# Second expert layer by row halves at full width, 12 tokens in a row per partition, and a renumbered planner table

## The chip, the cores and the metric

The kernel runs on one core of a Trainium2 chip, in one launch. The metric is device time in microseconds of that launch. Engines are named as the profile names them: PE multiplies matrices (PEld is its loading of the stationary operand), DVE and ACT are the vector and the scalar engine, POOL is the general one, and SP issues every transfer between HBM and the on-chip memory, on one queue.

## The reference

Sliding-window attention with four sink positions feeds a soft mixture of experts. There are 4 batches of 8 heads, 768 positions and 64 channels, so x has 3072 tokens of 512 channels; there are 8 experts with 4 slots each and 1024 hidden channels.

```python
scores = scale * np.matmul(q, k.transpose(0, 1, 3, 2))
keep = is_sink | in_window                     # first 4 positions, or the last 128
a = softmax(np.where(keep, scores, -1e9))      # over keys
x = (a @ v), laid out as (B * S, H * D)        # 3072 x 512
logits = x @ phi                               # 3072 x 32 slots
d = softmax(logits, over tokens)
slot_input = (d.T @ x).reshape(E, 4, D)
for e in range(E):
    slot_out[e] = np.maximum(slot_input[e] @ w1[e], 0.0) @ w2[e]
c = softmax(logits, over slots)
out = c @ slot_out                             # 3072 x 512
```

Everything is float32. The weights w1 and w2 are 16.8 MB each, and the output is 6.3 MB.

## The kernel before

**Two stages.** The attention stage walks over 12 jobs: batch b and a block j of 256 positions, three blocks to a batch. For a job it loads 256 positions of k, q and v (each in two transfers of 256 KB, called halves here), transposes k and q on PE, multiplies scores for four tiles, takes maxima on DVE and exponentials on ACT, normalises on POOL, transposes the result, masks it on POOL, multiplies it with v and with the sink values, and adds the block to the running sums of the slot inputs. The tail then multiplies the 32 slot inputs with w1, applies the rectifier, transposes, multiplies with w2 and combines for all tokens.

**Order.** The attention stage is written as a list of steps, each with a key, an engine, an estimated time, what it reads and what it writes. `Plan.order` (lines 165 to 246) replays the list on a model of five engines: of the steps of an engine that could start now it takes the one with the smallest key. The keys come from the table CFG (lines 671 to 690), most of them as 4n plus an entry for job n. The order found this way is the program order of each engine. For the queue "D", that is SP, the steps are the loads of k, q, v, the gate phi, the sink values v4, and 17 weight tiles. Weight step i has the key `O["w"][0] + O["w"][1] * i` (line 994) and depends on nothing; the loads of job n have keys `4.0 * n + O["load"][kind]` and `4.0 * n + O["v"][i]`. The k and q of job 0 are issued at line 1165, ahead of all this. The first products on PE are warm-up on the identity.

**Weights.** `Weights.load` issues one transfer of 1 MB (1,048,576 bytes) into a slot of 128 partitions x 2048 floats, in a fixed order of 32 tiles: 16 tiles of w1, then 16 of w2. A w1 tile has runs of 4 KB in HBM. A w2 tile is one expert with 256 of the 512 columns, so its runs are 1 KB; first the left halves of all eight experts, then the right ones. Tiles 1 to 17 go out in the attention stage (NSLOT is 24), one into the buffer first[0] when the last q and k have been used, four into slots as the attention stage frees them, one into first[1], and nine more from within the tail (`more`), as the w1 tiles are used up.

**Second layer and output.** The four experts of a row half r sit side by side in PE's four column groups of 32 (j), so four matmuls run at once; k counts the eight parts of the hidden channels. Before, the 512 output columns are done as three strips s0 (256 columns), s1 and s2 (128 each): for each strip 16 steps over r and k (`second`), a split of the result into a high part and a remainder (`split`), and the combination with the slot weights ct for 24 groups of 128 tokens (`combine`), four groups to a store. Group i holds tokens 128 i + p on partition p, so a store has runs of 1 KB (s0) or 512 B (s1, s2). `turned` transposes the last six units of ct between steps. Tiles of a strip's combination and steps of the next strip are interleaved by hand. An instruction that is issued through the ordering helper is recorded at line 127.

Of the kernel before, what the change touches and what calls it, by code (L numbers as in the profile page):

```python
# [8 lines left out]
F32 = mybir.dt.float32  # L9
# [5 lines left out]
ALU = mybir.AluOpType  # L15
# [4 lines left out]
P = 128  # L20
# [251 lines left out]
class Moe:  # L272
# [246 lines left out]
    def tail(self, slot, wts, more, out):  # L519
        nc, c, B, si, pool = self.nc, self.c, self.B, self.si, InOrder(self.pools)  # L520
# [40 lines left out]
        ops = [pool.tile("s") for _ in range(2)]  # L561
        tw = slot().bitcast(F32R)[:, 0:1024].rearrange("p (x m) -> p x m", x=2)
        obs = [slot() for _ in range(3)]
        ov = out.rearrange("(i p) m -> p i m", p=P)

        def op(s):
            return ops[s[0] == 256][:, s[0] > 256, 0:s[1]]

        def second(s, r, k0=0, k1=8):
            c0, m = s  # L570
            h, o = divmod(c0, 256)
            for k in range(k0, k1):
                for j in range(4):
                    nc.tensor.matmul(op(s)[32 * j:32 * j + 32],
                                     lhsT=ht[:, k, r, j].rearrange("p q i -> p (q i)"),
                                     rhs=wts[16 + 8 * h + 4 * r + j][:, 256 * k + o:256 * k + o + m],
                                     start=(r == 0 and k == 0), stop=(r == 1 and k == 7), skip_group_check=True)

        def split(s):
            c0, m = s  # L580
            hi, x = tw[:, 0, c0:c0 + m], op(s)
            nc.scalar.copy(hi, x)
            nc.vector.scalar_tensor_tensor(tw[:, 1, c0:c0 + m], hi.bitcast(F32), c.lo_rows, x,  # L583
                                           op0=ALU.mult, op1=ALU.add)

        def combine(s, n):
            c0, m = s
            per = 512 // m

            x = n + (6 if c0 == 384 else 0) if m == 128 else 2 * n  # L590
            x, y = divmod(512 * x, 2048)
            ob = obs[x][:, y:y + 4 * m].rearrange("p (i m) -> p i m", i=4)
            for x in range(4 // per):
                yp = pool.tile()
                for y in range(per):
                    i = 4 * n + per * x + y
                    nc.tensor.matmul(yp[:, m * y:m * y + m], lhsT=self.ct[i // 12][:, i // 6 % 2, i % 6, :],
                                     rhs=tw[:, 1, c0:c0 + m], start=(y == 0), stop=(y == per - 1),
                                     skip_group_check=True)
                (nc.scalar.copy if (n * (4 // per) + x) % 2 == 0 else nc.vector.tensor_copy)(  # L600
                    ob[:, per * x:per * x + per, :], yp.rearrange("p (i m) -> p i m", i=per))
            nc.sync.dma_start(ov[:, 4 * n:4 * n + 4, c0:c0 + m], ob)

        s0, s1, s2 = (0, 256), (256, 128), (384, 128)
# [5 lines left out]
        steps = {s: iter([(s, r, k, k + 1) for r in range(2) for k in range(8)]) for s in (s0, s1, s2)}  # L610

        def some(s, n):
            for _ in range(n):
                second(*next(steps[s]))

        def combined(s, *n):
            for x in n:
                combine(s, x)

        for n in range(3):  # L620
            some(s0, 4)
            turned(n)
        some(s0, 4)
        split(s0)
        some(s1, 4)
        combined(s0, 0, 1)
        some(s1, 3)
        turned(3)
        combined(s0, 2, 3)
        some(s1, 3)  # L630
        turned(4)
        combined(s0, 4)
        some(s1, 3)
        turned(5)
        some(s1, 3)
        split(s1)
        combined(s0, 5)
        some(s2, 4)
        combined(s1, 0, 1)
        some(s2, 4)  # L640
        combined(s1, 2, 3)
        some(s2, 4)
        combined(s1, 4)
        some(s2, 4)
        split(s2)
        combined(s1, 5)
        combined(s2, *range(6))


class Weights:  # L650


    def __init__(self, nc, w1, w2):
        self.nc, self.w1, self.tiles = nc, w1, []
        self.order = [(w1, 4 * r + 2 * j, k) for r in range(2) for k in range(4) for j in range(2)]
        self.order += [(w2, e, h) for h in range(2) for e in range(8)]

    def load(self, t):
        w, e, h = self.order[len(self.tiles)]
        first = w is self.w1  # L660
        self.nc.sync.dma_start(
            t.rearrange("p (k m) -> p k m", k=2 if first else 8),
            w[e:e + 2].rearrange("e (k p) m -> p e k m", p=P)[:, :, h, :] if first else
            w[e].rearrange("(p k) m -> p k m", p=P)[:, :, 256 * h:256 * h + 256])
        self.tiles.append(t)


NSLOT = 24
WARM = 8, 10
PT = 3  # L670
CFG = {'prep': [-1.63, -1.96],
       'load': [-6.04, -6.69],
       'v': [-6.3, 0.97],
       'S': -4.67,
       'M': 2.42,
       'E': -3.34,
       'N': 0.29,
       'K0': 1.89,
       'T': [2.6, 6.04, 3.99, 4.25],
       'K': 6.01,  # L680
# [543 lines left out]
```

## Time and profile before

| | us |
|---|---|
| median of 3 runs | 268.26 |
| lowest, highest run | 266.33, 268.53 |
| profiled execution | 266.88 |
| its span | 265.2 |
| attention stage, to the slot inputs (copy of si on DVE) | 0 to 205.1 |
| first layer of the experts on PE | 205.2 to 221.4 |
| last weight tile used from | 240.4 |
| last copy of an output tile ends | 257.2 |

The page gives an execution's busy times, a chain of work that ended last, and groups of instructions. Rows of busy time by stage give the start and end of a stretch, its length, the busy time of PE, PEld, DVE, ACT and POOL in it with the number of instructions, the granted clock of PE (1.00 is full), the mean busy share of the DMA engines and GB/s. Rows of the timeline give start, length, engine, line, operation, what is written and read, and, in brackets, how long the engine stood before and what released it. Rows of waits give the total, the number and the longest. Rows of transfers end with KB and the microseconds from issue to landing. A float32 matmul is recorded twice, once for each of its two passes.

| GB/s by the page's 40 slices | |
|---|---|
| slices 24 to 29 (152 to 192 us) | 42, 119, 77, 124, 2, 42 |
| slices 33 to 37 (212 to 245 us) | 348 to 354, then 318 |
| slices 38 to 40 (245 to 265 us) | 233, 248, 138 |

### The profile page before, as it was taken

The page shows a single profiled execution, that of the slowest core. Times are in us where ns is not written, and L with a number is a line of the kernel's source. Part 1 is how long each engine was busy: PE and PEld are TensorE (multiplying, and loading weights), DVE is VectorE, ACT ScalarE, POOL GpSimd, SP SyncE. Part 2 cuts the span into 40 slices and gives each one's busy share as a digit, 9 for nine tenths or more (in the row PEclk, how much of TensorE's full clock was granted, in tenths as well). Part 3 has the DMA queues.
Part 4 walks back from the last instruction along what each step waited for, and adds up shares of the span by engine and source line. Part 5 has one row for each costly group of instructions (what it writes and reads, how often), then busy time and mean ns, then how long its engine had stood idle before and what let it go on. Part 6 is the DMA issues. An engine that isn't in the chain of part 4 may idle for free.

```text
span 265.2 us, 7578 instructions
## 1 busy us (share of the span) xinstructions
PE 235.4 (89%) x2802; PEld 163.4 (62%) x2802; DVE 173.0 (65%) x449; ACT 147.7 (56%) x578; POOL 141.3 (53%) x280
## 2 busy tenths in 40 slices
PE   7777999979999997999999799998896999977960
PEld 7655686746767684676678566766574225555850
DVE  2287989698889869888986989898415213041340
ACT  2366877577686857678685767767633003142330
POOL 1145989684775958477695847669942040310000
PEclk9979999999999999999999999999998699997995
DMA  7998797988889898589889816340199799999784
GB/s 139 191 197 162 203 269 248 275 172 267 232 259 327 277 235 256 171 167 353 247 271 224 215 42 119 77 124 2 42 288 346 217 351 348 350 354 318 233 248 138
DMA packets 106111, 59.38 MB, mean 224 GB/s; under 512 B 76372, under 2 KB 101972, under 8 KB 106068
## 3 DMA queue, kind: packets, MB, share of 16 engines
q1 hardware_dynamic: 106068, 58.83, 79.5%
q8 instruction: 24, 0.39, 0.6%
q14 instruction: 19, 0.16, 0.2%
HBM read 52.53 MB, written 6.29 MB: 222 GB/s over the span
## 4 chain that ended last, share of the span: by engine, by line
PE 61%; DVE 19%; DMA 5%; ACT 5%; POOL 3%; issue 3%; ACTq 0%; POOLq 0%; DVEq 0%
PE w L127 47%; PE s L127 13%; DVE wt L127 7%; DVE s L127 6%; DMA wt<-in_moe_w_dram 5%; POOL wt L127 3%; ACT wt L127 2%; DVE sums L127 2%; PE w L1176 1%; ACT lt L127 1%; ACT qt L127 1%; DVE call L127 1%; DVE rs L127 1%; DVE acc L127 1%; DVE pst L127 1%
## 5 line engine op out<-in xcount | busy, mean ns | idle before, releaser
L127 POOL TENSOR_TENSOR wt<-wt 128x528 f32<-128x528 f32 (+1 forms) x96 | 64.5, 673 | 27.8 <-DVE wt L127 23.9
L127 ACT ACTIVATE wt<-s,wt 128x132 f32<-128x132 f32 x192 | 68.5, 378 | 11.5 <-DVE wt L127 10.4
L127 POOL TENSOR_SCALAR_AFFINE_SELECT wt<-wt 128x512 f32<-128x512 f32 x88 | 53.8, 635 | 24.5 <-DVE wt L127 15.3
L127 PE MATMUL w<-wt 128*64 128x128 f32 (+4 forms) x586 | 55.0, 315 | 0.3 <-DVE wt L583 0.2
L127 PEld LDWEIGHTS w<-wt 128*64 128x64 f32 (+2 forms) x586 | 40.3, 144 | 12.2 <-issue 1.1
L127 PE MATMUL s<-wt,qt 64*64 64x196 f32 (+2 forms) x768 | 43.7, 331 | 3.5 <-ACT wt L127 2.9
L127 PE MATMUL w<-ident,first 128*128 128x128 f32 x288 | 42.8, 281 | 3.7 <-DVE pst L127 2.8
L127 PE MATMUL w<-ident,wt 128*128 128x128 f32 x256 | 38.5, 280 | 2.9 <-POOL wt L127 2.3
L127 ACT ACTIVATION_READ_ACCUMULATOR wt<-s,wt 128x1 f32 x192 | 40.9, 213 | 0.0
L127 PEld LDWEIGHTS w<-ident,first 128*128 128x128 f32 x288 | 31.9, 142 | 12.2 <-issue 4.8
L127 PEld LDWEIGHTS s<-wt,qt 64*64 64x64 f32 x768 | 27.6, 135 | 15.7 <-ACT wt L127 8.4
L127 ACT COPY first<-w 128x512 f32<-128x512 f32 x36 | 21.2, 589 | 28.1 <-PE w L127 28.0
L127 PEld LDWEIGHTS w<-ident,wt 128*128 128x128 f32 x256 | 28.7, 145 | 10.8 <-POOL wt L127 4.7
L127 DVE TENSOR_REDUCE wt<-s 128x4 f32<-128x528 f32 x48 | 34.0, 707 | 1.6
L127 DVE COPY wt<-w 128x512 f32<-128x512 f32 x46 | 30.3, 682 | 1.9 <-PE w L127 1.7
L127 DVE COPY_PREDICATED s<-later,s 128x256 f32<-128x256 uint8 x48 | 20.3, 422 | 6.4 <-PE s L127 5.8
L127 PE MATMUL s<-wt 128*32 128x128 f32 (+1 forms) x352 | 18.1, 316 | 3.1 <-DMA wt<-in_moe_w_dram 3.1
L127 ACT COPY wt<-w 128x512 f32<-128x512 f32 x26 | 14.9, 593 | 6.2 <-PE w L127 6.0
L127 PE MATMUL w<-wt,si 128*32 128x512 f32 x128 | 16.2, 670 | 0.4 <-DVE si L127 0.4
L127 PEld LDWEIGHTS s<-wt 128*32 128x32 f32 x352 | 11.1, 114 | 7.6 <-DMA wt<-in_moe_w_dram 3.7
L600 DVE COPY wt<-w 128x512 f32<-128x512 f32 x12 | 8.1, 690 | 11.2 <-PE w L127 11.2
L127 DVE MEMSET s<- 64x512 f32 (+1 forms) x16 | 6.2, 385 | 14.0 <-PE s L127 13.3
(109 smaller groups left out, 243.2 us busy)
## 6 DMA issues: line engine op xcount, KB each, us to landing
wt<-in_moe_w_dram SPq DMA_DIRECT2D x30, 1024.0 KB, 7.9
first<-in_k_dram SPq DMA_DIRECT2D x24, 256.0 KB, 4.2
first<-in_q_dram SPq DMA_DIRECT2D x24, 256.0 KB, 4.3
wt<-in_v_dram SPq DMA_DIRECT2D x24, 256.0 KB, 4.2
out_dram<-wt SPq DMA_DIRECT2D x6, 512.0 KB, 5.1
out_dram<-wt SPq DMA_DIRECT2D x12, 256.0 KB, 4.4
first<-in_moe_w_dram SPq DMA_DIRECT2D x2, 1024.0 KB, 6.8
acc<-in_moe_phi_dram SPq DMA_DIRECT2D x1, 64.0 KB, 5.1
```

The costliest lines, as they stand in the source:

```text
L127: return self.tc.keep_in_program_order(f(*args, **kw))
L600: (nc.scalar.copy if (n * (4 // per) + x) % 2 == 0 else nc.vector.tensor_copy)(ob[:, per * x:per * x + per, :], yp.rearrange("p (i m) -> p ...
L1176: nc.tensor.matmul(t[:, 0:P], lhsT=c.ident, rhs=c.ident, start=True, stop=True)
```

## The change

**Second layer.** One accumulation of 128 partitions x 512 columns takes the place of the three strips: 16 steps of four matmuls with 512 columns (64 instructions in place of 192), the six turns of ct after every second step. The result is split in two halves of 256 columns once all steps are done, and the combination starts after that.

**Weight tiles.** The w2 tiles are now row halves: for r = 0 four experts with 8 KB runs (four of the eight parts k, all 512 columns), twice; for r = 1 the first four parts the same way, and the last four parts in four tiles that hold two experts and two parts each, in 4 KB runs. The number of tiles and their size are the same.

**Output.** The tokens of a group are now every twelfth one: partition p of a group i holds token 12 p + i of a half of 1536 tokens, so the stationary operand is `ct[:, i:1536:12]`, and a store of two or four groups has runs of 4 or 8 KB. There are seven stores in place of 18. Each group is two matmuls of 256 columns into one PSUM tile and one copy of 512 columns, on ACT and DVE in turn.

**The planner's table.** All entries of CFG but a few are renumbered. The weight steps' key goes from 9.75 + 16.41 i to 6.04 - 3.67 i; the other entries move the order of PE, DVE, ACT and POOL in the first four of the twelve jobs, and of a few steps later, most of them on POOL.

SP's queue after the branch, before (in_moe_w is w1 or w2, first holds q and k, wt is a slot, acc the gate's phi; "32x1x64" are the sink values):

```order
L127 DMA wt<-in_v_dram 128x8x64
L127 DMA first_76<-in_q_dram 128x8x64 x2
L127 DMA wt<-in_v_dram 128x8x64
L127 DMA first_76<-in_k_dram 128x8x64 x2
L127 DMA acc<-in_moe_phi_dram 128x4x32
L127 DMA wt<-in_v_dram 128x8x64
L127 DMA first_76<-in_q_dram 128x8x64 x2
L127 DMA wt<-in_v_dram 32x1x64 x4
L127 DMA first_76<-in_k_dram 128x8x64 x2
L127 DMA wt<-in_v_dram 128x8x64
L127 DMA first_76<-in_q_dram 128x8x64 x2
L127 DMA wt<-in_moe_w_dram 128x2x1024
```

The same queue from the same place, after:

```order
L127 DMA wt<-in_moe_w_dram 128x2x1024 x13
L127 DMA wt<-in_v_dram 128x8x64
L127 DMA wt<-in_moe_w_dram 128x2x1024
L127 DMA first_76<-in_q_dram 128x8x64 x2
L127 DMA wt<-in_v_dram 128x8x64
L127 DMA first_76<-in_k_dram 128x8x64 x2
L127 DMA wt<-in_moe_w_dram 128x2x1024
L127 DMA acc<-in_moe_phi_dram 128x4x32
L127 DMA first_76<-in_q_dram 128x8x64 x2
L127 DMA wt<-in_v_dram 128x8x64
L127 DMA wt<-in_v_dram 32x1x64 x4
L127 DMA first_76<-in_k_dram 128x8x64 x2
```

The first weight tile moved from the twelfth place to the first, and thirteen of them now stand ahead of job 0's v and job 1's q and k. The keys below those of job 0's loads are those with i from 4 to 16. All other loads keep their order except the sinks, which stand behind one more weight tile.

PE from the first value product of job 0 on, before (w<-wt 128x256 is the product that spreads the sink values, pst,vsink and wt 64x256 the value product; w<-ident,first are transposes of k or q, w<-ident,wt of exponentials, s<-wt,qt scores):

```order
L127 MATMUL w<-ident,first_76 128x128 x8
L127 MATMUL s<-wt,qt 64x196 x8
L127 MATMUL w<-wt 128x256
L127 MATMUL s<-wt,qt 64x196 x8
L127 MATMUL w<-ident,wt 128x128 x6
L127 MATMUL s<-wt,qt 64x196 x8
L127 MATMUL w<-pst,vsink 128x256 x2
L127 MATMUL w<-wt 64x256 x2
```

After:

```order
L127 MATMUL w<-ident,first_76 128x128 x4
L127 MATMUL s<-wt,qt 64x196 x8
L127 MATMUL w<-ident,wt 128x128 x10
L127 MATMUL w<-wt 128x256
L127 MATMUL w<-ident,first_76 128x128 x8
L127 MATMUL w<-pst,vsink 128x256 x2
L127 MATMUL w<-wt 64x256 x2
```

The four score tiles of job 1 and ten transposes now all stand ahead of the sink product, and between it and the value product stand the eight transposes of job 2's k.

SP's end of the queue, before:

```order
L127 DMA first_76<-in_moe_w_dram 128x8x256
L127 DMA wt<-in_v_dram 128x8x64 x2
L127 DMA wt<-in_moe_w_dram 128x8x256 x4
L127 DMA first_77<-in_moe_w_dram 128x8x256
L127 DMA wt<-in_moe_w_dram 128x8x256 x9
L602 DMA out_dram<-wt 128x4x256 x6
L602 DMA out_dram<-wt 128x4x128 x12
```

After:

```order
L127 DMA first_76<-in_moe_w_dram 128x2048
L127 DMA wt<-in_v_dram 128x8x64 x2
L127 DMA wt<-in_moe_w_dram 128x2048 x4
L127 DMA first_77<-in_moe_w_dram 128x2048
L127 DMA wt<-in_moe_w_dram 128x2048 x5
L127 DMA wt<-in_moe_w_dram 128x2x1024 x4
L606 DMA out_dram<-wt 128x1024 x2
L606 DMA out_dram<-wt 128x2048 x5
```

The weight tiles keep their places and change their shape; the stores are fewer and larger.

The diff, cut:

```diff
-        ops = [pool.tile("s") for _ in range(2)]
+        op = pool.tile("s")[:, 0, :]
...
-        def second(s, r, k0=0, k1=8):
-            c0, m = s
-            h, o = divmod(c0, 256)
-            for k in range(k0, k1):
-                for j in range(4):
-                    nc.tensor.matmul(op(s)[32 * j:32 * j + 32],
-                                     lhsT=ht[:, k, r, j].rearrange("p q i -> p (q i)"),
-                                     rhs=wts[16 + 8 * h + 4 * r + j][:, 256 * k + o:256 * k + o + m],
...
+        def second(r, k):
+            t = 16 + 8 * r + 4 * (k // 4)
+            for j in range(4):
+                if t < 28:
+                    w = wts[t + j][:, 512 * (k % 4):512 * (k % 4) + 512]
+                else:
+                    o = 1024 * (j % 2) + 512 * (k % 2)
+                    w = wts[28 + 2 * (k % 4 // 2) + j // 2][:, o:o + 512]
+                nc.tensor.matmul(op[32 * j:32 * j + 32], lhsT=ht[:, k, r, j].rearrange("p q i -> p (q i)"), rhs=w,
+                                 start=(r == 0 and k == 0), stop=(r == 1 and k == 7), skip_group_check=True)
...
+        for r in range(2):
+            for k in range(8):
+                second(r, k)
+                if k % 4 in (1, 3) and 4 * r + k // 2 < 6:
+                    turned(4 * r + k // 2)
+        for h in range(2):
+            o = slice(256 * h, 256 * h + 256)
+            hi, x = tw[:, 0, o], op[:, o]
+            nc.scalar.copy(hi, x)
+            nc.vector.scalar_tensor_tensor(tw[:, 1, o], hi.bitcast(F32), c.lo_rows, x, op0=ALU.mult, op1=ALU.add)
+        n = 0
+        for x in range(2):
+            ct = self.ct[x].rearrange("p b i y -> p (b i y)")
+            ov = out[1536 * x:1536 * x + 1536].rearrange("(p i) m -> p i m", i=12)
+            for i0, i1 in ((0, 2), (2, 4), (4, 8), (8, 12)) if x == 0 else ((0, 4), (4, 8), (8, 12)):
+                ob = slot()[:, 0:512 * (i1 - i0)].rearrange("p (i m) -> p i m", i=i1 - i0)
+                for i in range(i0, i1):
+                    yp = pool.tile()
+                    for h in range(2):
+                        o = slice(256 * h, 256 * h + 256)
+                        nc.tensor.matmul(yp[:, o], lhsT=ct[:, i:1536:12], rhs=tw[:, 1, o],
+                                         start=(h == 0), stop=(h == 1), skip_group_check=True)
+                    (nc.vector.tensor_copy if n % 2 else nc.scalar.copy)(ob[:, i - i0], yp)
+                    n += 1
+                nc.sync.dma_start(ov[:, i0:i1], ob)
...
-        self.order += [(w2, e, h) for h in range(2) for e in range(8)]
+        self.order += [(1, 4 * r + j, h) for r in range(2) for h in range(2 - r) for j in range(4)]
+        self.order += [(2, 4 + 2 * j, h) for h in (2, 3) for j in range(2)]
...
+        elif kind == 1:
+            t2, w = t, self.w2[e].rearrange("(p k) m -> p (k m)", p=P)[:, 2048 * h:2048 * h + 2048]
+        else:
+            t2 = t.rearrange("p (e m) -> p e m", e=2)
+            w = self.w2[e:e + 2].rearrange("e (p k) m -> p e (k m)", p=P)[:, :, 1024 * h:1024 * h + 1024]
...
-       'load': [-6.04, -6.69],
-       'v': [-6.3, 0.97],
+       'load': [-5.67, -7.5],
+       'v': [-6.3, 1.13],
...
-       'w': [9.75, 16.41],
+       'w': [6.04, -3.67],
```

More of the change, by code (lines that the diff above doesn't have):

```diff
@@ L558, in tail @@
                         tv[:, :, o:o + 4].unsqueeze(2).to_broadcast([P, 4, 4, 4]))
-        ops = [pool.tile("s") for _ in range(2)]
+        op = pool.tile("s")[:, 0, :]
         tw = slot().bitcast(F32R)[:, 0:1024].rearrange("p (x m) -> p x m", x=2)
[L563 to L567, printed above, removed]
-        def second(s, r, k0=0, k1=8):
-            c0, m = s
-            h, o = divmod(c0, 256)
-            for k in range(k0, k1):
-                for j in range(4):
-                    nc.tensor.matmul(op(s)[32 * j:32 * j + 32],
-                                     lhsT=ht[:, k, r, j].rearrange("p q i -> p (q i)"),
-                                     rhs=wts[16 + 8 * h + 4 * r + j][:, 256 * k + o:256 * k + o + m],
-                                     start=(r == 0 and k == 0), stop=(r == 1 and k == 7), skip_group_check=True)
@@ L579, in split @@
[L579 to L602, printed above, removed]
@@ L608, in turned @@
                 self.stack(pool, 0, *x)
[L610 to L647, printed above, removed]
+        for r in range(2):
[3 more added lines that the diff above has]
+                    turned(4 * r + k // 2)
@@ L650 @@
 class Weights:
     def __init__(self, nc, w1, w2):
-        self.nc, self.w1, self.tiles = nc, w1, []
-        self.order = [(w1, 4 * r + 2 * j, k) for r in range(2) for k in range(4) for j in range(2)]
-        self.order += [(w2, e, h) for h in range(2) for e in range(8)]
+        self.nc, self.w1, self.w2, self.tiles = nc, w1, w2, []
+        self.order = [(0, 4 * r + 2 * j, k) for r in range(2) for k in range(4) for j in range(2)]
+        self.order += [(1, 4 * r + j, h) for r in range(2) for h in range(2 - r) for j in range(4)]
@@ L658, in load @@
+        self.order += [(2, 4 + 2 * j, h) for h in (2, 3) for j in range(2)]
     def load(self, t):
[L659 to L664, printed above, removed]
+        kind, e, h = self.order[len(self.tiles)]
@@ L670 @@
 PT = 3
-CFG = {'prep': [-1.63, -1.96],
-       'load': [-6.04, -6.69],
-       'v': [-6.3, 0.97],
[L674 to L680, printed above, removed]
-       'sel': [-1.27, 3.49, 5.2, 5.63],
-       'val': [4.23, -3.12, 6.88, 6.2],
-       'xn': [4.41, 9.69],
-       'tok': [8.18, -3.3, 2.52, 9.73, -3.43, 2.02, 20.75, 8.54, -19.96, 9.83, 8.57, -3.96, -5.2],
-       'sm': 7.56,
-       'sinks': -17.8,
-       'tr': [82.74, 108.12, 84.87, 81.07, 78.87, 106.75, 100.27, 89.21, 88.74, 84.76, 75.82, 91.91, 78.76, 83.59, 95.74,
-              84.37, 80.06, 79.94],
-       'w': [9.75, 16.41],
-       'fin': [13.43, 15.87, 17.03, 13.9, 22.7, 30.28, 19.15, 31.22, 16.82]}
+CFG = {'prep': [-0.83, -2.01],
+       'load': [-5.67, -7.5],
+       'v': [-6.3, 1.13],
+       'S': -4.68,
+       'M': 2.64,
+       'E': -10.98,
+       'N': 0.37,
+       'K0': 2.2,
+       'T': [3.54, 5.68, 4.49, 4.82],
+       'K': 5.39,
+       'sel': [1.56, 3.55, 5.89, 5.5],
+       'val': [4.94, -2.24, 7.58, -3.62],
+       'xn': [3.77, 9.39],
+       'tok': [8.0, 1.25, -0.68, -2.13, -12.74, 2.36, 24.17, 9.57, -11.78, 9.75, 2.14, 0.07, 12.41],
+       'sm': 11.76,
+       'sinks': -17.32,
+       'tr': [89.91, 131.92, 88.37, 67.4, 63.94, 121.01, 102.28, 79.84, 107.91, 82.2, 75.98, 101.65, 80.5, 86.37, 104.75,
+              74.65, 82.33, 52.82],
+       'w': [6.04, -3.67],
+       'fin': [3.13, 27.1, -0.65, 30.1, 31.16, 8.6, 16.71, 33.78, 1.07]}
 def window_path(ctx, tc, c, moe, q, k, v, phi, w1, w2, out):
```

4 lines of the change are left out of this document (3 added, 1 removed).

## Prediction

> **What bounds the kernel now.** I read the page's busy times and chain first, then the busy time by stage, then what PE waited for, then SP's own rows, since SP issues every transfer.
>
> ```profile
> PE 235.4 (89%) x2802; PEld 163.4 (62%) x2802; DVE 173.0 (65%) x449; ACT 147.7 (56%) x578; POOL 141.3 (53%) x280
> ...
> PE 61%; DVE 19%; DMA 5%; ACT 5%; POOL 3%; issue 3%; ACTq 0%; POOLq 0%; DVEq 0%
> ```
>
> ```profile
> 10.00:30.00 20.00, 15.08 (x172) 10.37 (x172) 15.98 (x44) 11.82 (x55) 9.54 (x18) 0.91 1.03 214
> 30.00:50.00 20.00, 20.00 (x253) 14.97 (x254) 16.82 (x41) 14.39 (x62) 18.15 (x37) 1.00 0.78 224
> ```
>
> ```profile
> PE w L127 <- ACT lt L127: 2.9, 4, 0.8
> PE w L127 <- DVE pst L127: 2.8, 3, 0.9
> PE w L127 <- DVE wt L127: 1.6, 6, 0.4
> PE w L127 <- POOL wt L127: 0.8, 1, 0.8
> ```
>
> PE carries the chain and is busy almost without a break from 30 us on. The four rows of waits are all of PE's from 30 to 195 us: 8.1 us, none of them for a transfer. So from 30 to 195 us the time is PE's own work, and a weight tile that lands earlier there gives nothing. A stop of PE at the start cannot be made up later, except out of those 8.1 us.
>
> The last 60 us are another stage. There the chain leaves PE once, for a weight tile:
>
> ```profile
> 227.28 13.11 DMA wt<-in_moe_w_dram
> 240.43 1.04 PE s L127 x10
> ...
> 253.53 2.91 PE w L127 x24
> 256.46 0.69 DVE wt L600
> ```
>
> So the tail is set by the weight stream until 240.4, and by the rest of the second layer, the combination and the stores from there to 265.2: 24.8 us.
>
> **The start.** SP's rows of before, PE's, and what three transfers took to land:
>
> ```profile
> 5.05 0.48 SPq L127 DMA_DIRECT2D wt<-in_v_dram  x1
> 8.36 1.24 SPq L127 DMA_DIRECT2D first<-in_q_dram  x2
> ...
> 25.13 1.14 SPq L127 DMA_DIRECT2D wt<-in_moe_w_dram  x1
> ```
>
> ```profile
> 11.61 0.66 PE L127 MATMUL w<-ident,first 128*128 128x128 f32 x4
> ...
> 22.81 1.04 PE L127 MATMUL w<-ident,first 128*128 128x128 f32 x8
> ...
> 25.90 0.69 PE L127 MATMUL w<-wt 32*128 32x256 f32 x2
> ...
> 29.73 0.50 PE L127 MATMUL w<-pst,vsink 128*128 128x256 f32 x2
> ```
>
> ```profile
> first<-in_q_dram SPq DMA_DIRECT2D x2, 256.0 KB, 3.2
> ...
> wt<-in_moe_w_dram SPq DMA_DIRECT2D x2, 1024.0 KB, 13.2
> ...
> out_dram<-wt SPq DMA_DIRECT2D x1, 512.0 KB, 7.2
> ...
> out_dram<-wt SPq DMA_DIRECT2D x1, 512.0 KB, 3.1
> ```
>
> Before, job 1's queries are issued at 8.36, land 3.2 us later, and PE transposes them at 11.61; the first weight tile is issued at 25.13. Now thirteen weight tiles go out at 5 us, ahead of all that. The question is whether a load waits behind what was issued before it on this queue. The last two weight tiles, issued behind four others, took 13.2 us. The store issued at 234.54, behind the same tiles, took 7.2 us; one of the same size on an empty queue took 3.1. So it waits. For the rate I take:
>
> ```profile
> 7.00:8.00 1.00, 1.00 (x11) 1.00 (x11) 0.00 (x0) 0.39 (x1) 0.21 (x1) 1.00 1.33 219
> 8.00:9.00 1.00, 1.00 (x11) 0.96 (x9) 0.00 (x0) 0.58 (x2) 0.00 (x0) 1.00 0.54 88
> 29.00:30.00 1.00, 1.00 (x18) 0.69 (x18) 1.00 (x2) 0.75 (x3) 1.00 (x2) 1.00 1.04 418
> 44.00:45.00 1.00, 1.00 (x15) 0.68 (x12) 0.94 (x3) 0.37 (x2) 0.92 (x4) 1.00 1.05 406
> 211.50:238.00 26.50, 25.55 (x333) 13.03 (x322) 5.96 (x15) 6.51 (x19) 6.14 (x13) 1.00 1.08 348
> ```
>
> The columns end with granted clock, DMA share and GB/s. Loads of q, k and v (256 B runs) move at 219 GB/s: 1.2 us for 262,144 bytes. First-layer weight tiles (4 KB runs) fill the two rows of 418 and 406; the long row of 348 is second-layer tiles in 1 KB runs. I take 405 GB/s, the lower of the rows with the same runs: 2.59 us a tile; the ends are 418 (2.51) and 348 (3.01).
>
> The Trainium skill's page "DMA: Bandwidth & Descriptors" (Where 436 GB/s comes from) says that for loads the HBM side binds, at about 358 GB/s a core. By that rule fourteen tiles take 41.0 us and not 36.2; this trace's 418 in a full microsecond is above it, the 348 is not.
>
> Job 0's q and k are issued before the branch and the queue is empty of them and of one v at about 8.5 (share 0.54 in 8 to 9), so the weights' turn begins at 8.5 - 1.2 = 7.3. Thirteen tiles: 33.7, to 41.0. Then one v, one more weight tile and the first half of job 1's q: 1.2 + 2.6 + 1.2, to 46.0, and 1 us to be seen: 47.0. PE's order puts those transposes right behind two score tiles, so PE stands from about 11.6 to 47.0, and DVE, ACT and POOL run dry behind it.
>
> What is late next: SP still has the second q half, v, two k, weight tile 15, phi, two q, v, the four small sink loads and two k: 4.8 + 2.6 + 0.3 + 2.4 + 1.2 + 0.3 + 2.4 = 14.0, to 60.0 and seen at 61.0; the sink loads are seen at 58.6. The new order has the sink product, then the eight transposes of that k (1.0), then the first value product. By the sinks it starts at 58.6 + (29.73 - 25.90) = 62.4; by k at 62.0. I take 62.5, against 29.73: +32.8. By then PE is ahead by sixteen transposes it did later before (eight of job 1's attention weights, eight of k): 2 x 1.04 = -2.1. After the gap PE's clock is low: the stage of 10 to 30 us ran at 0.91, 1.8 us lost, behind one wait of 1.3 us; PE has hardly worked from 47 to 62, so +1.3 of at most 1.8. **The start costs +32.0** (ends: 418 GB/s makes it 30.8, 348 GB/s 38.3).
>
> From the fifth job on PE's rows are word for word the old ones, but for one place in the last job. I cost the rest of the renumbered table at nothing: what hides it is PE's own work, and if the other engines' changed order at the batch starts uncovers a wait, it is a part of the 8.1 us; ends -3 and +3.
>
> **The tail.** Rows:
>
> ```profile
> 211.34 0.12 PEld L127 LDWEIGHTS w<-wt,si 128*32 128x32 f32 x4 [0.31 <-issue]
> 211.77 0.12 PEld L127 LDWEIGHTS w<-wt,si 128*32 128x32 f32 x4 [0.31 <-issue]
> ...
> 225.22 0.44 PE L127 MATMUL w<-ident,wt 128*128 128x128 f32 x2
> ```
>
> ```profile
> 232.06 0.37 ACT L582 CAST wt<-s 128x256 fp32r<-128x256 f32 x1 [1.52 <-PE s L127]
> 232.46 0.48 DVE L583 SCALAR_TENSOR_TENSOR wt<-wt,lo_rows,s 128x256 fp32r<-128x256 f32 x1 [8.02 <-ACT wt L582]
> ...
> 242.98 0.69 DVE L600 COPY wt<-w 128x512 f32<-128x512 f32 x1 [5.79 <-PE w L127]
> ```
>
> ```profile
> 233.00 1.22 PE L127 MATMUL w<-wt 128*128 128x256 f32 x8
> ```
>
> ```profile
> 238.00:243.40 5.40, 3.09 (x30) 2.30 (x32) 0.42 (x1) 0.96 (x2) 0.00 (x0) 0.73 1.07 378
> 257.00:262.00 5.00, 0.00 (x0) 0.00 (x0) 0.15 (x1) 0.00 (x0) 0.00 (x0) 0.56 0.94 263
> ```
>
> All times here are on the old clock; the start shifts them together. Nine tiles issued from 208.86 took 26.5 us at 348 GB/s. Now they have 8 KB and 4 KB runs: at 405, 23.3 us, so the last lands at about 237.2 and not 240.4 (at 348: no gain; 8 KB runs are in no row).
>
> A 512-wide step of the second layer has the shape of a first-layer step: four instructions side by side, two passes, 2 x 0.43 = 0.86 at full clock. Sixteen steps from 223.4 are 13.8, six turns of ct 6 x 0.4 = 2.4: PE ends at 239.6, later than the last tile by more than its last two steps (1.7), so PE sets it, warm. Then the split of two halves, 0.37 + 0.48 + 0.48 = 1.3, to 240.9. The first store wants two token groups: four products of 0.15 and a copy of 0.69, 1.4, to 242.3, and 0.4 to issue. All 6.29 MB of stores now come behind this point: nothing is written before, where the old kernel had written 2.1 MB by 243.4. At 378 GB/s, the row of 1 KB runs, they take 16.6 us (418: 15.0; 263, the row of 512 B runs: 23.9); longer runs lie nearer the faster row. Copies are no bound: a group of 262 KB takes 0.69 us on either engine, two engines side by side, and its store 0.69. A 512 KB store on the empty queue took 3.1 to land and moves in 1.4 at this rate. With 3.1 - 1.4 = 1.7 for its start and landing and 1.3 from the last landing to the span's end (the last store, issued at 259.5, landed 4.4 later, the span ends at 265.2): 242.3 + 0.4 + 16.6 + 1.7 + 1.3 = 262.3. **The tail gives -2.9** (ends -5 and +4.4). Eleven fewer stores on SP save only issue time beside transfers.
>
> Sum: 266.88 + 32.0 - 2.9 = 296.0 for an execution like the profiled one, which lies 1.4 under the median of 268.26; half of that added, 296.7.
>
> **Rivals.** (1) *The stream runs at 348 whatever its runs.* For it: the longest full stretch. Against: 406 and 418 with these very tiles. Fifteen tiles x 0.42 = +6.3: 303.0. The skill's 358 of the page named above is this rival. (2) *PE catches up.* With most weights loaded, the attention stage has its queue to itself, and the new order may close all 8.1 us of waits: 288.6. Against: none of them is for a transfer. (3) *The stores crawl* at 263 when they all stand alone behind the last product: +7.3, 304.0. Against: that row has 512 B runs. (4) *Loads slip past the weights*, the other side: the queue serves the small loads between the tiles, job 1's q lands near 11.6, and only the tail's gain is left: 296.7 - 32.0 = 264.7. It decides if that q lands before 14.5, where the start's loss would equal the tail's gain. Against: the store that took 7.2 us. The skill's page "DMA: Bandwidth & Descriptors" (Rules for kernel authors) tells one to issue a DMA early and wait on it late. By that rule alone the early tiles are free, as in this rival; the 7.2 against 3.1 us says that what is queued behind pays.
>
> **How the numbers follow.** Forecast 0.62, rival 1 0.14, rival 2 0.12, rival 3 0.07, rival 4 0.05. The time is the forecast's, 296.7. From 288.0 to 305.0 the range takes in rivals 1 to 3 and leaves out rival 4 and what of 1 and 3 adds up, under 2 in 10. About 1% is what can be told from no change here: rival 4 is 1.1% under 267.6 (the profiled time with the same half added), so it splits into 0.03 faster and 0.02 within 1%; all else is slower, 0.95.
>
> **What would show it.** Right: PE idle from about 12 to 47 us on a load of q; DMA share full with about 405 GB/s from 7 to 41; the first value product near 62; PE without waits for transfers after; the second layer ending within 2 us of the last tile; one unbroken run of stores of about 17 us. Wrong: job 1's q landing before 20 us, a rate of 350 in the first 40 us, or stores under 300 GB/s.

## The result, and the profile after

| | before | changed |
|---|---|---|
| median of 4 runs each (us) | 267.62 (266.33 to 268.53) | 300.31 (299.49 to 301.94) |
| profiled execution, span (us) | 265.2 | 298.2 |

The changed kernel takes 1.1233 times as long (95% interval 1.1160 to 1.1306). The two spans are 33.0 us apart. One instruction divides the time into its two stages in both kernels: VectorE's copy of the gate's result si, with which the weight layers can start. VectorE's timeline has it here in the kernel before:

```profile
204.84 0.29 DVE L127 COPY si<-w 128x128 f32<-128x128 f32 x1 [1.27 <-PE w L127]
```

and here in the changed kernel (start, duration, then in brackets the idle time before it and what ended it):

```profile
239.48 0.29 DVE L127 COPY si<-w 128x128 f32<-128x128 f32 x1 [0.81 <-PE w L127]
```

Up to it the changed kernel loses 239.48 - 204.84 = 34.6 us. From it to the end it needs 298.2 - 239.48 = 58.7 in place of 265.2 - 204.84 = 60.4, and so wins 1.6.

**The start.** The page of the changed kernel: PE, clock, DMA share and GB/s in 40 slices of some 7.5 us, and the chain.

```profile
PE   7600005779999999997999997999988899998970
...
PEclk9965555999999999999999999999999979999795
DMA  8999999797674557184166285154114969990595
GB/s 151 397 409 411 409 373 234 200 265 203 138 162 88 113 102 144 35 178 109 43 136 135 47 164 118 39 106 144 37 36 167 397 203 424 418 365 5 209 413 233
...
PE 51%; DVE 18%; SPq 12%; DMA 5%; ACT 4%; POOL 4%; issue 3%; DVEq 0%; ACTq 0%; POOLq 0%
```

PE is empty in slices 3 to 6, just where the transfers run at their full rate, and its granted clock falls to 0.5 there. The chain now goes through SP's queue (SPq 12%), which had no share of it before. SP's timeline names the transfers:

```profile
4.98 20.75 SPq L127 DMA_DIRECT2D wt<-in_moe_w_dram  x13
25.78 3.62 SPq L127 DMA_DIRECT2D wt<-in_v_dram  x1
29.44 9.71 SPq L127 DMA_DIRECT2D wt<-in_moe_w_dram  x1
39.27 3.32 SPq L127 DMA_DIRECT2D first<-in_q_dram  x2
```

SP itself is held up: the issue of a weight tile that took 1.14 us before takes 9.71 here. Job 1's q, issued at 8.36 before, goes out at 39.27. Further on, SP issues job 2's two q at 49.80 and a v half and the four sink loads behind them at 52.27; before, that v half went out ahead of the two q (14.00 and 14.67). So the sinks are not the only small loads that moved, but no wait of PE hangs on this one. PE's timeline shows who waits for it, and how the work then comes back:

```profile
11.23 1.55 PE L127 MATMUL s<-wt,qt 64*64 64x196 f32 x30 [0.58 <-ACT qt L127]
47.71 1.08 PE L127 MATMUL w<-ident,first 128*128 128x128 f32 x4 [34.93 <-DMA first<-in_q_dram]
...
57.86 0.90 PE L127 MATMUL s<-wt,qt 64*64 64x196 f32 x16 [1.07 <-ACT wt L127]
...
64.27 0.66 PE L127 MATMUL w<-ident,wt 128*128 128x128 f32 x4 [0.69 <-POOL wt L127]
...
66.81 0.66 PE L127 MATMUL w<-ident,first 128*128 128x128 f32 x4 [0.68 <-ACT wt L127]
67.89 0.51 PE L127 MATMUL w<-pst,vsink 128*128 128x256 f32 x2 [0.41 <-DVE vsink L127]
```

One wait of 34.93 us is as long as the whole loss. Behind it, to the first value product at 67.89, no bracket names a transfer: the softmax chains of jobs 0 and 1 come through PE, ACT and POOL in turn.

**The tail.** Busy time by stretch (the last three columns are granted clock, DMA share and GB/s):

```profile
7.00:41.00 34.00, 5.20 (x61) 4.47 (x59) 4.44 (x12) 5.10 (x20) 2.35 (x5) 0.66 1.03 403
257.00:262.00 5.00, 5.00 (x44) 1.55 (x46) 0.98 (x6) 1.35 (x7) 0.89 (x3) 1.00 1.02 409
276.00:278.00 2.00, 1.81 (x7) 1.82 (x7) 0.82 (x2) 0.66 (x2) 0.00 (x0) 0.78 0.00 0
278.00:280.00 2.00, 2.00 (x9) 2.00 (x9) 1.16 (x3) 1.10 (x2) 0.00 (x0) 0.50 0.56 223
286.00:288.00 2.00, 2.00 (x9) 2.00 (x9) 1.26 (x2) 1.09 (x2) 0.00 (x0) 1.00 1.04 430
```

The second layer's tiles, now in 8 and 4 KB runs, stream at 409 GB/s (408 in the next 5 us) where 1 KB runs gave 348. Then nothing is moved until the first store, and the stores climb from 223 to 430 GB/s. The timeline of all engines over the join:

```profile
274.32 0.37 ACT L588 CAST wt<-s 128x256 fp32r<-128x256 f32 x1 [3.23 <-PE s L127]
...
276.19 12.87 PE L127 MATMUL w<-wt 128*128 128x256 f32 x47 [0.38 <-DVE wt L589]
276.77 0.58 ACT L604 COPY wt<-w 128x512 f32<-128x512 f32 x1 [1.15 <-PE w L127]
277.31 0.69 DVE L604 COPY wt<-w 128x512 f32<-128x512 f32 x1 [1.18 <-PE w L127]
277.93 0.59 ACT L604 COPY wt<-w 128x512 f32<-128x512 f32 x1 [0.58 <-PE w L127]
```

The combination's products take 12.87 / 47 = 0.27 us each, the copies wait for PE, and one copy follows another in some 0.54 us.

### The profile page after: what moved, and what is told of

Its sections match the earlier page's. It is cut to its first block, busy times and chain, and to the rows that moved or that the text cites. A ratio compares the mean times of both kernels' runs of the same rounds, so it can differ in the third digit from the quotient of the medians.

```text
span 298.2 us, 6972 instructions
## 1 busy us (share of the span) xinstructions
PE 238.2 (80%) x2522; PEld 159.9 (54%) x2522; DVE 171.7 (58%) x449; ACT 148.3 (50%) x576; POOL 141.2 (47%) x280
## 4 chain that ended last, share of the span: by engine, by line
PE 51%; DVE 18%; SPq 12%; DMA 5%; ACT 4%; POOL 4%; issue 3%; DVEq 0%; ACTq 0%; POOLq 0%
PE w L127 39%; PE s L127 12%; SPq L127 11%; DVE wt L127 8%; DMA first<-in_q_dram 5%; POOL wt L127 4%; DVE s L127 4%; ACT wt L127 3%; DVE call L127 1%; DVE rs L127 1%; DVE qt L127 1%; ACT lt L127 1%; DVE pst L127 0%; DVE acc L127 0%; DVE first L127 0%
## 5 line engine op out<-in xcount | busy, mean ns | idle before, releaser
L127 PE MATMUL w<-ident,first 128*128 128x128 f32 x288 | 43.4, 283 | 37.6 <-DMA first<-in_q_dram 34.9
L127 PE MATMUL w<-wt 128*64 128x128 f32 (+3 forms) x562 | 57.6, 329 | 1.4 <-DVE wt L589 1.4
L127 PEld LDWEIGHTS w<-wt 128*64 128x64 f32 (+2 forms) x562 | 44.1, 157 | 12.8 <-DVE wt L589 2.5
L127 PE MATMUL s<-wt,qt 64*64 64x196 f32 (+2 forms) x768 | 44.4, 330 | 2.5 <-ACT wt L127 1.7
L127 DVE COPY wt<-w 128x512 f32<-128x512 f32 x42 | 27.8, 683 | 3.0 <-PE w L127 2.6
L127 ACT COPY wt<-w 128x512 f32<-128x512 f32 x30 | 17.2, 592 | 8.1 <-PE w L127 8.0
L127 PE MATMUL w<-wt,si 128*32 128x512 f32 x128 | 15.5, 645 | 0.4 <-DVE si L127 0.4
L127 PE MATMUL s<-wt 128*32 128x512 f32 x112 | 15.2, 597 | 0.0
L127 DVE TENSOR_TENSOR wt<-wt 128x4 f32<-128x4 f32 x48 | 13.4, 279 | 2.9 <-ACT wt L127 2.7
L127 PE MATMUL w<-pst,vsink 128*128 128x256 f32 x48 | 12.0, 332 | 1.9 <-DMA first<-in_q_dram 1.4
```

Of the source, the lines that this page charges most:

```text
L127: return self.tc.keep_in_program_order(f(*args, **kw))
```

## Experiments

Where no interval stands, the time is that of one execution; a ratio is to runs of the kernel before on the same chip (266.6 to 267.4 in the median).

### The parts of the change apart

The old keys of the weight steps in the changed kernel:

```diff
-       'w': [6.04, -3.67],
+       'w': [9.75, 16.41],
```

> The changed kernel with one entry of the table put back: the weight steps' key is 9.75 + 16.41 i again, so job 0's v and job 1's q and k lead the queue and the first weight tile stands behind them. Theory (the thirteen tiles ahead of the loads make the whole loss): PE's wait of 34.9 us for job 1's q is gone, the slot inputs are done near 205 us, the tail keeps its small gain, and the time is 264 to 268 us. Rival (the rest of the table or the new tail loses time): 290 us or more.

Measured: 265.32 us, ratio 0.9912 (0.9881 to 0.9944). PE's rows for job 1's q, one for each half, are back:

```profile
11.81 0.66 PE L127 MATMUL w<-ident,first 128*128 128x128 f32 x4
13.68 0.63 PE L127 MATMUL w<-ident,first 128*128 128x128 f32 x4 [1.21 <-DMA first<-in_q_dram]
```

So two numbers of the table hold the whole loss, and without them the change is 0.9% faster. (The planner lays out the other engines anew when these numbers change; runs further down hold that fixed.) The other way round, the kernel before with that one line changed to the new keys:

> The kernel before with only the weight steps' key changed to 6.04 - 3.67 i; all else of its table and its tail stay. Theory: the same thirteen tiles lead the queue, PE waits some 35 us for job 1's q, and with the old tail the time is 300 to 304 us. Rival (the loss comes from the renumbered rest or from the tail): 266 to 275 us.

Measured: 303.13 us. The wait for q is there:

```profile
46.85 1.09 PE L127 MATMUL w<-ident,first 128*128 128x128 f32 x4 [34.03 <-DMA first<-in_q_dram]
```

And the new tail with the whole table of before:

> The changed kernel with the whole old table: only the second layer, the weight tiles' shapes, the combination and the stores are new. Theory (the tail gains a little, since the stream is faster but all stores stand behind the second layer): from the slot inputs to the end 58.5 to 59 us in place of 60.4, and 265 to 267 us in all. Rival (the tail's gain was hidden by its start in the stalled kernel and is worth 5 us or more here): 262 us or less. Other rival (it loses): 270 us or more.

Measured: 266.48 us, ratio 0.9969 (0.9952 to 0.9987). The tail by itself is worth 0.3%. All three times lie in their theory's range; from the copy of si to the end the last run took 59.2 us, a little over the 58.5 to 59 expected.

### The dose: how many tiles ahead

Nine tiles ahead in place of fourteen, by the slope of the key alone:

```diff
-       'w': [6.04, -3.67],
+       'w': [6.04, -1.2],
```

> The changed kernel with the weight steps' key 6.04 - 1.2 i: nine tiles, not fourteen, stand ahead of job 1's q, and thirteen, not fifteen, ahead of the sink values. Theory (a load waits for every byte issued before it on the queue, 2.59 us a tile): PE sees job 1's q 13 us earlier, near 34.5 us, and the time falls by 10 to 13 us to 287 to 290. Rival (the wait is a fixed cost of a full queue, whatever stands in it): within 3 us of 300.

Measured: 298.47 us, a miss, though q landed as it should. The time lies in the rival's range, but not for the rival's reason: a fixed cost of a full queue would have left q where it was, and PE saw it 12.9 us earlier. PE's timeline:

```profile
15.62 0.98 PE L127 MATMUL s<-wt,qt 64*64 64x132 f32 x16 [3.52 <-ACT wt L127]
...
34.83 1.11 PE L127 MATMUL w<-ident,first 128*128 128x128 f32 x4 [13.40 <-DMA first<-in_q_dram]
40.90 2.03 PE L127 MATMUL w<-ident,first 128*128 128x128 f32 x8 [1.96 <-DMA first<-in_k_dram]
...
56.66 0.67 PE L127 MATMUL w<-wt 32*128 32x256 f32 x2 [2.17 <-DMA wt<-in_v_dram]
```

The key also moved the steps of the other engines, since the planner lays out all queues together, and new waits took the place of the old one. A key can't be the dose here. The next two kernels keep the changed kernel's order on PE, VectorE, ScalarE and GpSimd instruction for instruction, and only hold back SP's first weight issues:

```diff
+            def go(e):
+                nc.sync.dma_start(t, (k, q, v)[kind][b, :, s0:s0 + P, :].rearrange("h p d -> p h d"))
+                if kind == 0 and n >= 2 and held[0]:
+                    held[0] -= 1
+                    weights.load(slot())
...
+        calls[0] += 1
+        if calls[0] <= 13:
+            held[0] += 1
+        else:
+            weights.load(slot())
```

> The changed kernel, its own table and its own order on PE, VectorE, ScalarE and GpSimd; only SyncE differs: the 13 weight tiles that led its queue are issued later, one behind each half-load of k from job 2 on. Theory (a load waits for the bytes that the queue took before it): PE's wait for job 1's q shrinks from 34.9 us to under 3, the first value product stands near 30 us, the span falls by 30 to 34 us and the time is 265 to 271. Rival (the renumbered table's order on the other engines costs by itself, since it was laid out around late loads): the wait for q goes, but value products and transposes wait elsewhere and the time is 275 or more.

Measured: 272.42 us, 1.4 above the range of the theory and under the rival's 275. With `<= 8` in place of 13:

> As the run before it, with 8 of the 13 tiles held back and 5 still ahead of job 1's q. Theory: each tile ahead costs 2.59 us, so q is seen 8 x 2.59 = 20.7 us earlier than at 47.7, at about 27 us, PE's wait for it is about 14 us, and the time is about 300.3 - 20.7 = 279.6 (277 to 283). Rival (the table's order has a price that does not go with the bytes): the wait shrinks as said, the time stays over 285.

Measured: 286.51 us. PE's timeline has the wait to a few tenths of what was expected:

```profile
27.18 1.09 PE L127 MATMUL w<-ident,first 128*128 128x128 f32 x4 [14.31 <-DMA first<-in_q_dram]
```

but the time is 7 above 279.6, in the rival's range. From no tile held to eight held, q comes 47.71 - 27.18 = 20.5 us earlier (8 x 2.56) and the time falls by 13.8; from eight to thirteen it falls by another 14.1, for 13.65 us of q. The landing of q goes with the bytes ahead of it. The time follows q only to within some 7 us; both runs are single executions.

### What the 7 us are

The suspects were tiles between the loads of jobs 2 to 6 (the run with 13 held still has waits of 2.5 us for k, 1.3 for v, 2.8 for q) and the order of the other engines. First the same kernel with `n >= 5` in place of `n >= 2`:

> The changed kernel with its table and its order on the other engines, 13 weight tiles held back as in the run that held all 13 (272.4 us), but given out from job 5 on in place of job 2, one behind each half-load of k. It settles what the 7 us are that this run stood above the old weight keys (265.3): Theory (tiles put between the loads of jobs 2 to 6 make those loads late: k 2.5 us, v 1.3, q 2.1 of waits on DMA there, and a granted clock of 0.91 from 50 to 70 us): with the tiles later the waits on DMA fall to under 2 us in all and the time is 264.5 to 268. Rival (the renumbered table's order on the other engines costs them): the waits go and the time stays 270 to 273.

Measured: 269.69 us (267.10 to 270.98), ratio 1.0115 (1.0075 to 1.0156): between the two, and wider spread than any other kernel. Three tiles still stood among the loads of jobs 0 to 2 there, issued at 5.67, 14.30 and 26.27. With all 16 held until job 4 (`<= 16`, `n >= 4`):

> The changed kernel with its order on PE, VectorE, ScalarE and GpSimd, and all 16 tiles held back and given out behind the half-loads of k from job 4 on: SyncE's first 21 steps are then word for word those of the run with the old weight keys, and the rest nearly so. It tells what the 4 us are by which the run with 13 held until job 5 stood above the old weight keys in the median (269.7 against 265.3). Theory (three tiles were still ahead of, or among, the loads of jobs 0 to 2 there, and their bytes are the cost): no wait on DMA above 1.5 us is left, and the time is 264.5 to 266.5. Rival (the order that the renumbered table gives the other engines costs 3 to 5 us by itself): the first value product stays near 34 us in place of 29.7, and the time is 268 to 271.

Measured: 271.31 us, ratio 1.0167 (1.0121 to 1.0214). PE's timeline, with no wait for q at all:

```profile
12.12 0.63 PE L127 MATMUL w<-ident,first 128*128 128x128 f32 x4
15.66 0.94 PE L127 MATMUL s<-wt,qt 64*64 64x132 f32 x16 [2.91 <-ACT wt L127]
...
36.25 0.51 PE L127 MATMUL w<-pst,vsink 128*128 128x256 f32 x2 [0.42 <-DVE vsink L127]
```

SP's queue begins as with the old keys, and the one load that PE waits for more than 1 us is a v (1.3). The time, 0.3 above the rival's range, is 1.0167 / 0.9912 = 2.6% over that with the old keys, some 7 us. It would seem that these are the same 7 us and that the planner's order for late loads costs them. The profiled executions say otherwise (us; PE's order is the same in the first five rows):

| run | job 1's q on PE | first value product | copy of si | from q to that copy |
|---|---|---|---|---|
| changed | 47.71 | 67.89 | 239.48 | 191.8 |
| 8 held, given out from job 2 | 27.18 | 47.50 | 226.20 | 199.0 |
| 13 held, given out from job 2 | 13.53 | 34.13 | 211.43 | 197.9 |
| 13 held, given out from job 5 | 13.50 | 34.69 | 206.69 | 193.2 |
| 16 held, given out from job 4 | 12.12 | 36.25 | 210.94 | 198.8 |
| old keys | 11.81 | 29.72 | 204.33 | 192.5 |
| before | 11.61 | 29.73 | 204.84 | 193.2 |

With tiles given out from job 2 on, the loss stands behind the first value product: from there to the copy of si it is 178.7 and 177.3 us, in place of 171.6 in the changed kernel. The loads behind those tiles are late. With eight held, PE waits 4.2 us for k and v after 50 us, and its granted clock is low around the longest of these waits:

```profile
65.19 0.63 PE L127 MATMUL w<-ident,first 128*128 128x128 f32 x4 [3.14 <-DMA first<-in_k_dram]
```

```profile
50.00:70.00 20.00, 16.78 (x185) 11.03 (x179) 10.51 (x26) 11.02 (x45) 10.56 (x22) 0.91 1.05 279
```

Given out from job 5 on, the tiles cost none of this (172.0). So the 7 us of the run with eight held are mostly the price of where the held tiles were put, as the theory of the run held until job 5 had it, and not a term of the changed kernel.

With all 16 held the loss stands ahead of the first value product, at 36.25 in place of 29.72, and there the rival's sign is seen. But of the 6.6 us to the copy of si, 4.5 are PE being busy longer with the same work (185.8 us in place of 181.4, from 8 us on) and only 2.2 are idle time. The granted clock goes with that; with the old keys,

```profile
14.00:30.00 16.00, 12.53 (x137) 8.14 (x135) 13.70 (x39) 11.68 (x55) 9.40 (x17) 0.89 0.98 208
30.00:50.00 20.00, 20.00 (x253) 14.97 (x254) 16.68 (x41) 14.47 (x62) 18.17 (x37) 1.00 0.79 227
```

and with all 16 held:

```profile
14.00:30.00 16.00, 12.50 (x116) 8.93 (x116) 12.54 (x34) 10.77 (x49) 7.47 (x13) 0.79 0.63 133
30.00:50.00 20.00, 17.90 (x188) 11.98 (x190) 15.09 (x38) 13.12 (x56) 14.63 (x28) 0.91 0.48 124
```

The run held until job 5 has the same order of PE, kept 0.89 and 1.00 in these stretches, and pays 0.7 us from q to the copy of si (its q is another 1.7 us late, behind the first of the three tiles). That execution is the fastest of its four, and their times go with their mean clock (267.10 at 0.967, 270.98 at 0.949). So the same order cost 0.7 us where the clock held and 6.3 where it fell. Why it fell was not tried: the wait of 2.91 us for ACT's softmax stands ahead of it, and waits of 1.7 and 2.1 us at that place in the runs with 13 held were followed by a full clock from 20 to 30 us, but no run changed this wait alone.

### Another queue

The changed kernel with all tiles still first on SP, and the loads of jobs 0 to 2, phi and the sink values issued elsewhere. The line for q, k and v; those for phi and the sinks go the same way:

```diff
-            add(key, "D", 1.35, lambda e: nc.sync.dma_start(
+            add(key, "D", 1.35, lambda e: (nc.scalar if n < 3 else nc.sync).dma_start(
```

> The changed kernel with all 16 weight tiles still first on SyncE, but the loads of jobs 0 to 2, phi and the sink values issued from ScalarE's queue. Theory (one queue hands its transfers to the DMA engines in order, so that what is behind the tiles waits for all of them): on a queue of their own the loads of job 1 share the engines with the tiles and land after about as many tile bytes as their own, 1 MB of q and k against 1 to 4 tiles; PE's wait for q falls from 34.9 us to 5 to 15, loads of job 3 are then the late ones (behind 16 tiles on SyncE, near 55 us), and the time is 270 to 290. Rival (what is late is set by the bytes in all, whatever the queue): q still lands after 35 us and the time stays within 297 to 302.

Measured: 306.66 us, slower than either theory. ScalarE's timeline shows why this could not tell them apart:

```profile
23.62 0.43 ACTq L127 DMA_DIRECT2D wt<-in_v_dram  x1
24.10 0.58 ACT L127 COPY wt<-w 128x512 f32<-128x512 f32 x1 [14.19 <-DMA wt<-in_moe_w_dram]
...
28.85 6.55 ACTq L127 DMA_DIRECT2D first<-in_q_dram  x2
```

ScalarE stood for 14 us at its first issue, with its copies behind it, and q went out at 28.85 only, to be seen by PE at 50.06. The bracket names a weight tile; why ScalarE's own queue stood so long is not shown. The same with GpSimd's queue (`nc.gpsimd`):

> The changed kernel with all 16 tiles first on SyncE and the loads of jobs 0 to 2, phi and the sink values on GpSimd's queue, where they can be issued from about 10 us on (ScalarE's queue gave job 1's q out at 28.9 us only, and it was seen at 50.1). Theory A (what is late waits in order behind the tiles of its own queue): q lands within 5 to 10 us of its issue, PE's wait for it is under 12 us, and the time is 268 to 288. Theory B (a transfer on another queue gets only a small share of the 16 engines while the tiles stream, so the tiles' bytes decide whatever the queue): q is seen at 40 to 50 us, PE waits over 25 us and the time is 295 to 308.

Measured: 293.96 us. GpSimd's timeline has q's issue:

```profile
10.80 1.76 POOL L127 DMA_DIRECT2D first<-in_q_dram  x2
```

and PE's what came of it:

```profile
19.33 1.08 PE L127 MATMUL w<-ident,first 128*128 128x128 f32 x4 [7.78 <-DMA first<-in_q_dram]
...
36.76 1.09 PE L127 MATMUL w<-ident,first 128*128 128x128 f32 x4 [3.64 <-DMA first<-in_q_dram]
48.55 0.63 PE L127 MATMUL w<-ident,first 128*128 128x128 f32 x4 [3.52 <-DMA first<-in_k_dram]
...
68.19 1.09 PE L127 MATMUL w<-ident,first 128*128 128x128 f32 x4 [4.70 <-DMA first<-in_q_dram]
```

Theory A is right on the landing (q is seen 8.5 us after its issue) and wrong on the time; theory B is wrong on the landing, and its time starts 1 us above what was measured. What held q in the changed kernel is its own queue's order. But past that queue, each load shares the 16 DMA engines with the tiles and takes about 8 us in place of 3, so the one long wait becomes several short ones (20.6 us for q and k in all). Of the 14 us of waiting that are saved only 6 are won: from 8 us to the copy of si PE is busy 193.2 us in place of 183.9 with the same work, and its granted clock is 0.76 from 30 to 70 us. The Trainium skill's page "DMA: Bandwidth & Descriptors" (Issuing engines are not separate DMA queues) says the same: transfers from any engine end up on the same 16 DMA engines and interleave. Both runs agree: q took 8.3 us to land from GpSimd's queue and 11.2 from ScalarE's (medians of four), against 3.2 before.

### The combination's weight load

The stationary operand as 128 columns in a row:

```diff
-                        nc.tensor.matmul(yp[:, o], lhsT=ct[:, i:1536:12], rhs=tw[:, 1, o],
+                        nc.tensor.matmul(yp[:, o], lhsT=ct[:, 128 * i:128 * i + 128], rhs=tw[:, 1, o],
```

> The changed kernel with the stationary operand of the combination read as 128 columns in a row in place of every twelfth one; the rows of the output then hold other tokens than they should (part of the computation changed: which token stands in which row). Theory (the stride of 12 is what makes the weight load of a product of the combination 369 ns on average in place of 198): the mean of these 48 loads falls under 0.2 us at the clock granted there, copies follow one another in 0.35 to 0.45 us in place of 0.535, and the stretch from the first product to the last store shortens by 0.5 to 1.5 us; the time stays 298.5 to 301. Rival (the load is as long because of the granted clock or the 32-bit operand): loads stay over 0.3 us and the cadence over 0.5.

Measured: 300.59 us. The groups of weight loads in the stretch of the combination (count, busy time, mean ns of one), changed kernel:

```profile
L127 PEld LDWEIGHTS w<-wt 128*128 128x128 f32 x48 | 13.0, 369 | 2.5 <-DVE wt L589 2.5
```

and without the stride:

```profile
L127 PEld LDWEIGHTS w<-wt 128*128 128x128 f32 x48 | 7.9, 226 | 4.0 <-DVE wt L589 2.6 <-ACT wt L604 0.9
```

The load falls to 0.61 of itself, not quite to the 0.2 expected, and the 47 products take 9.22 us in place of 12.87. From the last second-layer product (276.0) to the end it is 22.9 us, against 23.9 in the changed kernel: 1.0 us, within the expected half to one and a half. What this kernel leaves out is the order of the tokens: its output rows hold other tokens than they should. Then as a whole kernel: old weight keys, four tokens in a row per partition (still 8 KB), sorted when the transposes are copied out of PSUM:

```diff
+            ct = self.ct[x].rearrange("p b i y -> p (b i y)").rearrange("p (g i q) -> p g i q", g=3, i=4)
+            ct = ct[:, n // 2, :, 64 * (n % 2):64 * (n % 2) + 64]
...
-                self.ct[x][:, b % 2, 2 * u:2 * u + 2, :], h["tile"][:, 0:256].rearrange("p (i y) -> p i y", i=2))
+                ct, h["tile"][:, 0:256].rearrange("p (q i) -> p i q", i=4))
...
+                        nc.tensor.matmul(yp[:, o], lhsT=ct[:, t:t + 128], rhs=tw[:, 1, o],
```

> The new tail with the old weight keys, and the combination's stationary operand laid out so that its 128 columns stand in a row: four tokens in a row per partition, sorted when the transposes are copied out of PSUM, stores still of 4 and 8 KB runs. Theory (the stride of the weight load was what held the combination's pace, worth 1.1 us from the end of the second layer to the end where the stride was simply left out): copies follow each other in 0.45 to 0.5 us in place of 0.535, and the time is 263.3 to 265.0, against 265.3 for the same without it and 267.4 before. Rival (the stores are the bound of the tail's end, or the sorted copies cost what the loads save): 265 to 266.5.

Measured: 265.00 us, ratio 0.9918 (0.9895 to 0.9942). The weight loads are short here too (227 ns), the copies follow each other in some 0.39 us, and from the last second-layer product to the end it is 23.0 us, against 23.9 with the old keys alone. In the time, against 0.9912 for the same without this edit, no gain can be told; the first value product of this profiled execution stands at 31.18 in place of 29.72, and whether the edit has a part in that is not shown. Both are faster than the kernel before and than the changed kernel; they are the best versions found.

## Why the prediction was right

**The queue.** Job 1's q was to be seen at 47.0 and was at 47.71; PE was to stand from 11.6 and stood from 12.8. The rate of 405 GB/s was 403 over 34 us, so rival 1 (348 throughout) falls, and with it the figure of 358 that the prediction took from the Trainium skill's page "DMA: Bandwidth & Descriptors" (Where 436 GB/s comes from): the measurement decides. That it is the bytes ahead, at 2.56 us a tile, is shown by the run with eight held back, and that it is the two keys alone by the first two runs.

**The start's +32.0.** It measured +34.6. Of the 2.6 between them, 0.7 is the queue: q came 36.1 us later than before, with 35.4 forecast. The other 1.9 is what followed. From q to the copy of si the forecast won back 3.4 us, and measured are 1.5 (191.8 us in place of 193.2). Inside that stretch two misses partly cancel, which is luck. The first value product, forecast at 62.5, stood at 67.89: the working took the loads of the sinks and of k as what is late next and allowed 15.5 us from q on, but the rows above have no wait on a load there. The kernel before took 18.1 us for it, the changed one 20.2, with PE busy for 16.5 of them: the engines' own work between q and that product, which the forecast did not count. The loss of 38.2 at that point (67.89 - 29.73) then shrank by 3.5 to the copy of si, where the working had 0.8: 2.1 for the transposes done ahead, less 1.3 for the clock. The clock's term was too large: PE ran at 0.90 over these 20.2 us, against 0.91 over the 18.1 before, which makes some 0.4.

**The rest of the table, costed at nothing.** Under this stall it cost nothing that shows: from q to the copy of si the changed kernel is no longer than the kernel before. But the reason given, that PE's own work hides it, was wrong in general: taken without the stall, the same order cost 6.3 us in the run with all 16 tiles held, and 0.7 where the clock held.

**The tail's -2.9.** It measured -1.6. The weight stream at 405 was 409 (the row that the 405 was taken from says 406). The nine tiles had landed by about 268 us, 233 on the old clock, with 237.2 forecast. So the sign that the second layer would end within 2 us of the last tile did not come: it ended some 6 us behind it. This cost nothing, since PE set the end, as forecast. That the second layer, forecast to end at 239.6 on the old clock, ended there to a tenth (274.3 - 34.6 = 239.7) is luck in part: it began 0.8 earlier than forecast and took 0.8 longer. The first store came 1.1 late (278.07 - 34.64 = 243.4 against 242.3), and two terms were mis-sized. One is the product of 0.15 us, taken from stationary columns in a row: with a stride of 12 it took 0.27. That is 0.5 of the 1.1, since without the stride the first store follows the second layer in 3.3 us in place of 3.8. The other is the split, which ended 1.9 us behind the second layer, with 1.3 forecast: the second half's cast started at 275.24, released by the first half's remainder on VectorE, which ended at 275.21. (The 1.4 for the first two groups adds up to 1.3 from its own terms, and the products without the stride took 0.20.) The stores then took 20.1 us to the end of the span, with 20.0 forecast: faster at their best than the 378 assumed (430), slower in their first 4 us. Rival 3 falls.

**The sum.** +34.6 - 1.6 = 33.0 in the spans, against 32.0 - 2.9 = 29.1 forecast; the error of 3.9 is 2.6 of the start and 1.3 of the tail. Rival 2 (PE catches up the 8.1 us of waits) falls for the most part: the rows of its waits from 70 to 228 us still add up to 6.2 us, 1.9 less than before. The forecast of 296.7 is 3.6 under the measured 300.31. Rival 4 (loads slip past) falls in the changed kernel, and the GpSimd run shows that even a queue of their own doesn't make early tiles free.

## What to carry to other kernels

A bulk load that nobody needs for 200 us is not free at the head of the queue: cost it as its bytes divided by the rate, charged to the first small load behind it that an engine waits for. Moving the small loads to another queue splits that wait but doesn't remove it; issuing the bulk later does, if it isn't put among the next small loads that are needed soon. Where a planner orders all engines from one table, a changed load time changes the other engines too, so test a dose by holding the other orders fixed. And before two losses of the same size are called one, look at where in the trace each of them stands, and at the granted clock there.

## What the runs showed of the hardware

A stationary operand of 32-bit columns read with a stride of 12 loads in 369 ns on average, and in 226 ns with the columns in a row. Long runs pay on both directions with one core at work: loads at 403 to 409 GB/s in 4 and 8 KB runs, stores at 422 and 430 in their best stretches of 2 us. With the first loads on GpSimd's queue PE had several waits of 3 to 8 us, and its granted clock was 0.76 from 30 to 70 us, where it was 1.00 in the kernel before. And the same 3.77 MB of small loads went as 15248 packets through ScalarE's queue and as 1280 through GpSimd's.
